# Fused attention and two feed-forward blocks on one Trainium2 core: other places in the order for weight conversions, a constant row and the splits of the values

## The chip, the cores and the metric

One core of one Trainium2 chip. The metric is the device time of one execution in microseconds (us); lower is better. Before the change it was 958.23 us, the median of three runs (957.24 to 959.21).

## The reference

Attention with rotary positions on 4 batches x 8 heads x 576 tokens x 64, then a gated block (512 to 1024, split into u and v, v normalised and mixed over the tokens), then a block with a low-rank mixing over the tokens (U: 576x32, V: 32x576) and a 512-2048-512 pair of layers. All is float32.

```
q_rot, k_rot = (rotate(q), rotate(k))
scores = scale * np.matmul(q_rot, k_rot.transpose(0, 1, 3, 2))
scores = scores - np.max(scores, axis=-1, keepdims=True)
attn = np.exp(scores)
attn = attn / (np.sum(attn, axis=-1, keepdims=True) + 1e-09)
attn_out = np.matmul(attn, v)
...
h = gelu_tanh(x @ w_in)
u, v = (h[..., :d_ff // 2], h[..., d_ff // 2:])
v_n = (v - mu) / np.sqrt(var + 1e-06) * g_ln
v_s = np.einsum('ts,bsd->btd', w_sg, v_n) + b_sg[None, :, None]
x = x + (u * v_s) @ w_out
...
u = x + (x.transpose(0, 2, 1) @ U @ V).transpose(0, 2, 1)
out = u + np.maximum(u @ w_ch1, 0.0) @ w_ch2
```

## The kernel before

Every float32 product is built from two TensorE operands of a shorter format: a high part (ScalarE copies the tensor into it) and a low part (the tensor less its high part). The weights arrive as 64-bit floats and are converted in place by `from_f64` (L66): one ScalarE operation (Abs) and four VectorE operations (L72 to L75) per chunk, then a ScalarE copy for the high part and a GpSimd subtraction for the low part.

**The attention** is written out by hand on all five engines. It runs in slots: slot t does the scores of chunk t % 5 of head t // 5 (`scores`: keys in chunks of 128, all 576 queries), the values product of slot t - 3 (`values`), row maxima 12 slots ahead (`row_max`), and then whatever was put down for slot t by `later`. 32 heads make 160 slots; some 20 slots lie before slot 0. Each engine does its part of the slots in order.

- Scores are two matmul pairs per chunk: one tile pair stacks a high part over a low one, the other (65 rows) pairs a high part with a low one, and its 65th row is -1 against the row of the maxima, so that the maximum is subtracted on TensorE. Before, tile K2 is `rot - K1` over all 128 partitions (L166), which overwrites the row of -1, so a memset on GpSimd (L172) writes it again for each head.
- For head h: rope on GpSimd in slots 5h-26, 5h-25 and 5h-23 (L147 to L149), the high part on ScalarE with a DMA in 5h-20 (L161, L163), the low part on GpSimd with two DMAs in 5h-17 (L166 to L168), the memset in 5h-11 (table `LEAD`).
- `row_max`: VectorE reduces scores in PSUM to a maximum (L220, five per head); there are three PSUM tiles for these and the scores together.
- Chunk 4 has 64 keys: its exponentials (L251) are split into a high part (L253, ScalarE) and a low part `ph` (L255, VectorE), and so are its values (`value_stacks`, L180 on ScalarE and L181 on GpSimd, per head).
- After the second head of pair i, from slot t0 = 10i + 12 on (`finish`): the row sums are collected by DMA (t0), 1e-9 is added on GpSimd (`guard`, L306, t0+5), VectorE inverts (L309, t0+7), two DMAs spread the result (t0+8, t0+11), and VectorE multiplies both heads (`apply`, L324, t0+24 and t0+26) (table `INVERSE`).
- Eight chunks of w_in, one of U and two of V are loaded 10 slots apart from slot 15 on (`MATRIX`, `APART`), and converted 15 slots after their load (`CONVERT`): Abs, then VectorE's four operations in four successive slots, then the high and the low part.

**Behind the attention** only TensorE's order is written by hand; a scheduler places the others. The gated block of batch 0 has v steps, u steps, four s steps (token mixing; their result g goes through VectorE L622 and L623, ScalarE L624, GpSimd L506), the v steps of batch 1, and four o steps (output matmul `w`, residual on VectorE L634), then the transposes `t` (L646) of the low-rank mixing, which is the first to use U4 and V4. `other_weights` (L522) converts w_out in four pieces, one per `next(ow)`; its raw tiles borrow the buffers YH and YL of the later steps.

Of the kernel before, what the change touches and what calls it, by code (L numbers as in the profile page):

```python
# [52 lines left out]
def tile_kernel(ctx: ExitStack, tc: tile.TileContext, qk, vv, tabs, w_in, g_ln, wsgT, b_sg, w_out, u_r, v_r, w1, w2, out):  # L53
# [123 lines left out]
    def value_stacks(h):  # L177
        VS = VSs[h % 4]
        src = VVs[(h // 2) % 3][:, SPLIT, h % 2, :D]
        later(max(NC * h - SPLIT_V[0], SPLIT_V_FIRST[0]), lambda: nc.scalar.activation(VS[:, 0, :, :D], src, AF.Copy))  # L180
        later(max(NC * h - SPLIT_V[1], SPLIT_V_FIRST[1]), lambda: (nc.gpsimd if h > 1 else nc.vector).tensor_tensor(VS[:, 1, :, :D], src, f(VS[:, 0, :, :D]), ALU.subtract))  # L181

    def first_stacks(h):
# [11 lines left out]
        def high():  # L195
            e = BY_ACT[h]
            copy(e[0], Q1[z], rot[z])
            copy(e[1], Q1[a], rot[z])
            copy(e[2], K1[a], rot[a])
            copy(e[3], K1[z], rot[a])  # L200
            copy(e[4], Q2[a, 0:S], rot[z])
# [713 lines left out]
```

## Time and profile before

| | |
|---|---|
| time, median of 3 runs | 958.23 us (957.24 to 959.21) |
| the profiled execution: its time | 957.72 us |
| its span in the profile | 955.9 us |
| granted TensorE clock, mean | 0.989 of full speed |
| TensorE busy (matmul) | 927.9 us, 97% |
| weight loads | 784.5 us, 82% |
| VectorE busy | 542.5 us, 57% |
| ScalarE busy | 346.8 us, 36% |
| GpSimd busy | 409.9 us, 43% |

The span is the part of the profiled execution that the profiler covers; its own time is 1.8 us longer. A matmul counts as busy while it waits in the pipe for an operand or for PSUM, so 97% is not the share of useful work. The attention takes about the first 311 us; VectorE's and GpSimd's work lies mostly there.

### The profile page before, as it was taken

What the parts mean: (1) busy time and instruction counts of PE and PEld (TensorE: products, weight loads), DVE (VectorE), ACT (ScalarE), POOL (GpSimd) and SP (SyncE); (2) the same over time, 40 slices, a digit from 0 to 9 for tenths busy, and PEclk for the clock granted to TensorE, in tenths of its full rate; (3) what the DMA queues carried; (4) which work ended last, traced back from release to release, by engine and by line L of the source; (5) the groups of instructions that cost most, each with busy time, mean ns of one, the idle gap of its engine ahead of it and who ended that gap; (6) DMA issues with size and microseconds to landing.
All of it is one profiled execution on the core that took longest, in us unless ns stands there. A gap on an engine that the chain in (4) does not pass through costs nothing.

```text
span 955.9 us, 13163 instructions
## 1 busy us (share of the span) xinstructions
PE 927.9 (97%) x5179; PEld 784.5 (82%) x5180; DVE 542.5 (57%) x721; ACT 346.8 (36%) x550; POOL 409.9 (43%) x352
## 2 busy tenths in 40 slices
PE   5899999999999999999999899999999999999998
PEld 2588777777887888999999787888888888888887
DVE  7766899999874486334338845642642552222222
ACT  4356666666656443313225322311220320101000
POOL 7787999999943485231417533210210220000000
PEclk7899999999999999999999999999999999999999
DMA  5477776776630500000003001320220210000112
GB/s 176 127 206 201 210 206 182 207 191 173 168 90 14 164 25 1 1 1 19 5 23 111 22 23 46 109 67 1 88 88 1 67 45 0 1 1 23 45 48 86
DMA packets 57301, 77.93 MB, mean 82 GB/s; under 512 B 29756, under 2 KB 33111, under 8 KB 57239
## 3 DMA queue, kind: packets, MB, share of 16 engines
q1 hardware_dynamic: 56928, 77.01, 28.7%
q8 instruction: 41, 0.67, 0.3%
q14 instruction: 22, 0.17, 0.1%
q10 hardware_dynamic: 310, 0.08, 0.0%
HBM read 55.02 MB, written 4.79 MB: 63 GB/s over the span
## 4 chain that ended last, share of the span: by engine, by line
PE 74%; DVE 17%; issue 3%; DMA 2%; POOL 2%; ACT 1%; SPq 0%; ACTq 0%; DVEq 0%; POOLq 0%
PE a L542 21%; PE r L542 20%; PE pv L272 10%; PE st L244 6%; PE w L542 5%; DVE MX L220 4%; PE m L542 3%; PE sm L215 3%; PE u L542 3%; PE v L542 3%; DVE ph L255 2%; DVE t L74 1%; DVE t L72 1%; DVE X L324 1%; DVE t L75 1%
## 5 line engine op out<-in xcount | busy, mean ns | idle before, releaser
L272 PE MATMUL pv<-pc,VV 128*65 128x288 f32 x512 | 144.7, 405 | 0.5 <-DVE sums L293 0.5
L220 DVE TENSOR_REDUCE MX<-sm 128x1 f32<-128x576 f32 (+1 forms) x160 | 117.6, 751 | 36.5 <-PE sm L215 33.6
L244 PE MATMUL st<-Q,K 65*128 65x288 f32 (+3 forms) x640 | 126.5, 320 | 1.6 <-DVE MX L220 1.2
L735 DVE SCALAR_TENSOR_TENSOR RL<-r,RH 128x1024 fp32r<-128x1024 f32 (+1 forms) x38 | 42.3, 1112 | 123.8 <-ACT RH L734 123.7
L734 ACT ACTIVATE RH<-r 128x1024 fp32r<-128x1024 f32 (+1 forms) x38 | 35.6, 936 | 207.2 <-PE r L542 207.2
L244 PEld LDWEIGHTS st<-Q,K 65*128 65x128 f32 (+3 forms) x640 | 95.6, 179 | 16.2 <-DVE MX L220 5.4
L750 DVE TENSOR_TENSOR X<-a,X 128x256 f32<-128x256 f32 (+4 forms) x65 | 46.4, 745 | 90.8 <-PE a L542 90.7
L247 ACT ACTIVATE pc<-st 128x576 f32<-128x576 f32 x128 | 82.8, 648 | 36.5 <-PE st L244 31.1
L542 PE MATMUL a<-RH,setB 128*128 128x512 f32 (+1 forms) x320 | 93.3, 368 | 0.0
L272 PEld LDWEIGHTS pv<-pc,VV 128*65 128x65 f32 x512 | 68.5, 136 | 29.5 <-DVE sums L293 0.7
L215 PE MATMUL sm<-K,Q 128*128 128x288 f32 (+1 forms) x320 | 76.8, 325 | 12.8 <-ACT Q L191 6.9
L542 PE MATMUL a<-RH,setA 128*128 128x512 f32 (+1 forms) x288 | 83.8, 367 | 0.0
L542 PE MATMUL r<-UH,setA 128*128 128x512 f32 (+1 forms) x256 | 73.1, 364 | 0.1
L542 PE MATMUL r<-UH,setB 128*128 128x512 f32 (+1 forms) x256 | 73.2, 363 | 0.0
L215 PEld LDWEIGHTS sm<-K,Q 128*128 128x128 f32 (+1 forms) x320 | 52.5, 184 | 20.2 <-ACT Q L191 7.4
L542 PEld LDWEIGHTS a<-RH,setB 128*128 128x128 f32 x320 | 58.2, 189 | 10.0
L506 POOL TENSOR_TENSOR setB<-t,setB 128x512 fp32r<-128x512 f32 x16 | 20.7, 1294 | 102.9 <-ACT setB L695 91.8
L542 PEld LDWEIGHTS a<-RH,setA 128*128 128x128 f32 x288 | 52.1, 188 | 9.0
L542 PE MATMUL a<-RL,setB 128*128 128x512 f32 (+1 forms) x160 | 58.9, 368 | 0.0
L148 POOL TENSOR_TENSOR raw<-raw,tab 128x576 f32<-128x576 f32 x31 | 54.5, 1760 | 5.6 <-DMA raw<-in_qk 5.6
L506 POOL TENSOR_TENSOR setA<-t,setA 128x512 fp32r<-128x512 f32 x16 | 21.5, 1352 | 73.7 <-ACT setA L695 69.9
L542 PEld LDWEIGHTS r<-UH,setA 128*128 128x128 f32 x256 | 46.1, 188 | 8.2 <-DVE X L676 0.4
(170 smaller groups left out, 2030.3 us busy)
## 6 DMA issues: line engine op xcount, KB each, us to landing
raw<-in_qk SPq DMA_DIRECT2D x31, 576.0 KB, 4.8
raw<-in_w SPq DMA_DIRECT2D x24, 512.0 KB, 3.6
Q<-K SPq DMA_DIRECT2D x29, 288.0 KB, 3.5
VV<-in_vv SPq DMA_DIRECT2D x16, 320.0 KB, 3.9
rb<-rr SPq DMA_DIRECT2D x15, 288.0 KB, 3.7
Q<-K SPq DMA_DIRECT2D x29, 144.0 KB, 2.4
K<-K SPq DMA_DIRECT2D x29, 144.0 KB, 2.4
raw<-in_w_in SPq DMA_DIRECT2D x8, 512.0 KB
```

Source lines behind the costliest of these rows:

```text
L148: lambda: e.tensor_tensor(raw[:, 1], raw[:, 1], tab[:, 1], ALU.mult),
L215: nc.tensor.matmul(ps[:TS[t], n, :HALF], Q1[:, t * P:t * P + TS[t]], K1[:, n * HALF:(n + 1) * HALF], start=True, stop=True)
L220: nc.vector.tensor_reduce(MXs[h % 2][:TS[t], t:t + 1], ps[:TS[t], :, :HALF], AX.XY, ALU.max)
L244: nc.tensor.matmul(ps[:kk, n, :HALF], l[:, c * P:c * P + kk], r[:, ns], start=st, stop=not st)
L247: nc.scalar.activation(h2(pc[:kk]), ps[:kk, :, :HALF], AF.Exp, scale=0.125)
L255: lows.append(lambda: nc.vector.tensor_tensor(ph[D:], pt, f(ph[:D]), ALU.subtract))
L272: nc.tensor.matmul(o, l, r, start=(c == 0 and j == 0), stop=(c == NC - 1 and j == len(pr) - 1))
L506: return nc.gpsimd.tensor_tensor(out, a, b, ALU.subtract)
L542: nc.tensor.matmul(o, l, rr, start=(j == 0), stop=(j == n - 1))
L734: nc.scalar.activation(RH[:, s], ps[:, :, :WIDE[blk]], AF.Relu)
L735: nc.vector.scalar_tensor_tensor(RL[:, s], ps[:, :, :WIDE[blk]], 0.0, f(RH[:, s]), ALU.max, ALU.subtract)
L750: nc.vector.tensor_tensor(X[b][:, e2, xs], ps[:, :n, us], X[b][:, e2, xs], ALU.add)
```

## The change

- Chunks of w_in stand 15 slots apart (`APART` 10 to 15), and only they are converted in the attention. U and V are converted in the gated block, as three more steps of `other_weights`: U with the fourth s step of batch 0, V's halves with the first two v steps of batch 1.
- k and q change roles: the kept tile with 65 rows (K2) now holds a high part that comes by DMA into 64 rows, and its row of -1 stays, so the memset per head is gone from head 5 on. The low part goes to Q2, whose 65th row is then overwritten by the row of maxima.
- The values of chunk 4 are split for both heads of a pair at once.
- The 1e-9 is added on VectorE, directly ahead of the inversion.
- A pair whose multiplications would fall into the slots of a chunk's conversion (`BUSY`) is multiplied at t0+19 and t0+21 in place of t0+24 and t0+26.

```diff
-LEAD = 26, 25, 23, 20, 17, 11
+LEAD = 26, 25, 23, 20, 17
...
-INVERSE = 5, 7, 8, 11, (24, 26)
+INVERSE = 7, 8, 11, (24, 26), (19, 21)
-MATRIX, APART, CONVERT, ROWS = 15, 10, 15, (151, 159)
+MATRIX, APART, CONVERT, ROWS = 15, 15, 15, (151, 159)
...
-    K1s = [p1.tile([P, S], F32R, name=f"K1_{i}") for i in range(NS)]
-    Qs = [p1.tile([P, S + NC * P], F32R, name=f"Q_{i}") for i in range(NS)]
-    Q1s = [t[:, :S] for t in Qs]
-    Q2s = [t[:D + 1, S:] for t in Qs]
-    K2s = [p1.tile([P, S], F32R, name=f"K2_{i}") for i in range(NS)]
+    Q1s = [p1.tile([P, S], F32R, name=f"Q1_{i}") for i in range(NS)]
+    Ks = [p1.tile([P, 2 * S], F32R, name=f"K_{i}") for i in range(NS)]
+    K1s = [t[:, :S] for t in Ks]
+    K2s = [t[:D + 1, S:] for t in Ks]
+    Q2s = [p1.tile([P, NC * P], F32R, name=f"Q2_{i}") for i in range(NS)]
...
         def low():
-            nc.gpsimd.tensor_tensor(K2, rot, f(K1), ALU.subtract)
-            nc.sync.dma_start(f(Q1[z]), f(K2[z]))
-            nc.sync.dma_start(f(K1[z]), f(K1[a]))
+            nc.gpsimd.tensor_tensor(Q2[:, :S], rot, f(Q1), ALU.subtract)
+            nc.sync.dma_start(f(K1[z]), f(Q2[z, :S]))
+            nc.sync.dma_start(f(Q1[z]), f(Q1[a]))
...
-            steps = rope(nc.gpsimd, h) + (high, low, lambda: nc.gpsimd.memset(f(K2[D:D + 1]), -1.0))
+            steps = rope(nc.gpsimd, h) + (high, low)
+            if h < NS:
+                steps += lambda: nc.gpsimd.memset(f(K2[D:]), -1.0),
...
     def value_stacks(h):
-        VS = VSs[h % 4]
-        src = VVs[(h // 2) % 3][:, SPLIT, h % 2, :D]
+        if h % 2:
+            return
+        VS = VSs[h // 2 % 2]
+        src = VVs[(h // 2) % 3][:, SPLITS[0], :, :D]
...
-        def guard():
-            nc.gpsimd.tensor_scalar_add(rc, rc, 1e-9)
-
         def invert():
+            nc.vector.tensor_scalar_add(rc, rc, 1e-9)
             nc.vector.reciprocal(rc, rc)
...
-                later(t0 + (INVERSE[4][a] if i < NP - 2 else 16 + a), lambda a=a: apply(a))
+                tick = t0 + INVERSE[4 if t0 + INVERSE[3][0] in BUSY else 3][a]
+                later(tick if i < NP - 2 else t0 + 16 + a, lambda a=a: apply(a))
...
-    def u_chunk(t0):
...
-    def v_chunk(t0, a):
...
+    BUSY = {MATRIX + APART * i + CONVERT + j for i in range(2 * KT) for j in range(1, 5)}
...
+        t = staged(p2, u_r, "YH", n=NC * 32).rearrange("p (c r) -> p c r", r=32)
+        for j in (0, 2, 3):
+            nc.scalar.activation(U4[:, :, j], t, AF.Copy)
+        less(U4[:, :, 1], t, f(U4[:, :, 0]))
+        yield
+        for a in range(2):
+            hs = slice(a * HALF, (a + 1) * HALF)
+            t = staged(p2, v_r[:, 2 * a * HALF:2 * (a + 1) * HALF], ("YL", "YH")[a], n=HALF)
+            nc.scalar.activation(V4[:, hs], t, AF.Copy)
+            less(V4[96:, hs], t[96:], f(V4[96:, hs]))
+            yield
...
-        run(v_step, n, 0, 1)
+        for t in range(2):
+            v_step(n, t)
+            next(ow, None)
```

GpSimd's order over two heads in the middle of the attention, before (raw is the rope's tile, setA a weight, VS the values' split, K the tiles of k):

```order
L172 MEMSET K_3_107 1x576
L147 TENSOR_TENSOR raw_89<-raw_89,tab 128x576
L148 TENSOR_TENSOR raw_89<-raw_89,tab 128x576
L350 TENSOR_TENSOR setA_74<-t_155,setA_73 128x512
L149 TENSOR_TENSOR raw_89<-raw_89 128x576
L306 TENSOR_SCALAR rc_1303<-rc_1303 128x9
L166 TENSOR_TENSOR K_0_104<-raw_92,K_0_94 128x576
L181 TENSOR_TENSOR VS_114<-VV_111,VS_114 128x64
```

The second head is the same without the lines of setA and rc. Now a head with a chunk and one without:

```order
L147 TENSOR_TENSOR raw_92<-raw_92,tab 128x576
L148 TENSOR_TENSOR raw_92<-raw_92,tab 128x576
L352 TENSOR_TENSOR setA_76<-t_147,setA_75 128x512
L149 TENSOR_TENSOR raw_92<-raw_92 128x576
L166 TENSOR_TENSOR Q_4_108<-raw_91,Q_4_98 128x576
L147 TENSOR_TENSOR raw_89<-raw_89,tab 128x576
L148 TENSOR_TENSOR raw_89<-raw_89,tab 128x576
L149 TENSOR_TENSOR raw_89<-raw_89 128x576
L166 TENSOR_TENSOR Q_0_104<-raw_92,Q_0_94 128x576
L185 TENSOR_TENSOR VS_114<-VV_111,VS_114 128x2x64
```

The memset and the sums' addition (rc) are gone, the values' split comes once for two heads, and a weight's subtraction once for three. On VectorE the slots of the table give over six heads: chunk, pair, pair, chunk, neither, pair; before it was chunk and pair in turn.

VectorE's order in the gated block of batch 0, from the last w_out piece to the statistics of batch 1's first v tiles, before (t is a tile being converted, g the gated product, m the s step's PSUM):

```order
L75 SCALAR_TENSOR_TENSOR t_3779<-YL,t_3779 128x512
L622 SCALAR_TENSOR_TENSOR g<-m_3_3788,gh,bh 128x576
L623 TENSOR_TENSOR g<-g,ug 128x576
L585 BN_STATS bst<-gt 128x6 x2
L586 BN_AGGR bmv<-bst 128x2 x2
```

and now, where two L75 of 128x288 and then the statistics follow the last row:

```order
L72 TENSOR_SCALAR t_3726<-t_3726 128x160
L73 TENSOR_SCALAR t_3726<-t_3726 128x160
L74 SCALAR_TENSOR_TENSOR t_3726<-YH,t_3726 128x160
L618 SCALAR_TENSOR_TENSOR g<-m_3_3691,gh,bh 128x576
L75 SCALAR_TENSOR_TENSOR t_3726<-YH,t_3726 128x160
L619 TENSOR_TENSOR g<-g,ug 128x576
L72 TENSOR_SCALAR t_3751<-t_3751 128x288
L72 TENSOR_SCALAR t_3790<-t_3790 128x288
L73 TENSOR_SCALAR t_3751<-t_3751 128x288
L73 TENSOR_SCALAR t_3790<-t_3790 128x288
L74 SCALAR_TENSOR_TENSOR t_3751<-YL,t_3751 128x288
L74 SCALAR_TENSOR_TENSOR t_3790<-YH,t_3790 128x288
```

Three operations of U stand ahead of the last g, one inside it, and all eight of V behind it, ahead of the statistics. ScalarE's order at the same place, now (GH is the high part of g, gt the gelu of v; before, the rows of U, t and V were not there):

```order
L510 ACTIVATE WOH<-t_3682 128x512
L515 ACTIVATE U_79<-t_3726 128x5x32 x3
L620 ACTIVATE GH<-g 128x576
L71 ACTIVATE t_3751<-YL 128x288
L71 ACTIVATE t_3790<-YH 128x288
L529 ACTIVATE gt<-v_0_3737 128x1024
L521 ACTIVATE V_80<-t_3751 128x288
L521 ACTIVATE V_80<-t_3790 128x288
L589 ACTIVATE VH<-gt 128x512 x2
```

GpSimd has the subtraction of U ahead of the low part of the last g, and those of V ahead of the variance of the v tiles.

## Rows read from the trace of the kernel before

**Rows 1.** Busy time of each engine in stretches: us, then engines, clock, DMA share, GB/s.
```profile
150.00:200.00 50.00, 49.38 (x289) 38.89 (x290) 49.50 (x61) 32.33 (x57) 48.44 (x41) 1.00 0.75 202
...
340.00:368.00 28.00, 25.98 (x160) 23.57 (x158) 25.91 (x26) 11.73 (x21) 20.26 (x14) 1.00 0.00 1
```

**Rows 2.** Timeline of ScalarE: the exponential of chunk 4, heads 0, 8, 22 and 28.
```profile
40.76 0.64 ACT L251 ACTIVATE pt<-st 64x576 f32<-64x576 f32 x1 [0.95 <-PE st L244]
...
108.61 0.64 ACT L251 ACTIVATE pt<-st 64x576 f32<-64x576 f32 x1 [1.12 <-PE st L244]
...
233.64 0.64 ACT L251 ACTIVATE pt<-st 64x576 f32<-64x576 f32 x1 [1.12 <-PE st L244]
...
284.54 0.64 ACT L251 ACTIVATE pt<-st 64x576 f32<-64x576 f32 x1 [1.12 <-PE st L244]
```

**Rows 3.** Timeline of TensorE's weight loads, 180 to 190 us, those that waited.
```profile
184.81 0.46 PEld L272 LDWEIGHTS pv<-ph,VS 128*65 128x65 f32 x4 [0.48 <-DVE ph L255]
185.60 0.57 PEld L244 LDWEIGHTS st<-Q,K 128*128 128x128 f32 x4 [0.33 <-DVE MX L220]
188.62 0.45 PEld L244 LDWEIGHTS st<-Q,K 128*64 128x64 f32 x4 [0.41 <-DVE MX L220]
```

**Rows 4.** VectorE's groups by form, 100 to 270 us: busy us, mean ns, idle before.
```profile
L220 DVE TENSOR_REDUCE MX<-sm 128x1 f32<-128x576 f32 x78 | 57.3, 752 | 5.4 <-PE sm L215 4.4
L255 DVE TENSOR_TENSOR ph<-pt,ph 64x576 fp32r<-64x576 f32 x20 | 31.5, 1574 | 0.6
L324 DVE TENSOR_TENSOR X<-stage,rb 64x576 f32<-64x576 f32 x19 | 22.7, 1193 | 0.3
...
L72 DVE TENSOR_SCALAR t<-t 128x512 f32<-128x512 f32 x7 | 10.6, 1508 | 0.0
L75 DVE SCALAR_TENSOR_TENSOR t<-raw,t 128x512 uint32<-128x512 uint32 x7 | 7.3, 1046 | 0.0
L73 DVE TENSOR_SCALAR t<-t 128x512 uint32<-128x512 uint32 x7 | 7.1, 1014 | 0.0
...
L74 DVE SCALAR_TENSOR_TENSOR t<-raw,t 128x512 uint32<-128x512 uint32 x7 | 4.7, 675 | 0.0
...
L72 DVE TENSOR_SCALAR t<-t 128x160 f32<-128x160 f32 x1 | 1.5, 1504 | 0.0
...
L73 DVE TENSOR_SCALAR t<-t 128x288 uint32<-128x288 uint32 x2 | 0.9, 451 | 0.0
L73 DVE TENSOR_SCALAR t<-t 128x160 uint32<-128x160 uint32 x1 | 0.8, 782 | 0.0
L75 DVE SCALAR_TENSOR_TENSOR t<-raw,t 128x160 uint32<-128x160 uint32 x1 | 0.7, 675 | 0.0
L74 DVE SCALAR_TENSOR_TENSOR t<-raw,t 128x160 uint32<-128x160 uint32 x1 | 0.3, 317 | 0.0
```

**Rows 5.** Timelines of VectorE and of GpSimd, 55 to 95 us.
```profile
84.65 0.75 DVE L255 TENSOR_TENSOR ph<-pt,ph 64x576 fp32r<-64x576 f32 x1
...
86.35 1.41 POOL L166 TENSOR_TENSOR K<-raw,K 128x576 fp32r<-128x576 f32 x1 [1.81 <-ACT K L161]
```

**Rows 6.** GpSimd's groups by form, 100 to 270 us: busy us, mean ns, idle before.
```profile
L350 POOL TENSOR_TENSOR setA<-t,setA 128x512 fp32r<-128x512 f32 x7 | 12.5, 1790 | 0.0
L172 POOL MEMSET K<- 1x576 f32 x20 | 11.4, 572 | 1.2
...
L306 POOL TENSOR_SCALAR rc<-rc 128x9 f32<-128x9 f32 x9 | 5.9, 659 | 0.8
```

**Rows 7.** Timeline of TensorE's weight loads, 365 to 402 us, two that waited.
```profile
370.00 0.30 PEld L542 LDWEIGHTS w<-GL,WOH 128*128 128x128 f32 x2 [1.51 <-POOL GL L506]
381.25 1.40 PEld L646 LDWEIGHTS t<-ident,X 128*128 128x128 f32 x13 [0.76 <-DVE X L634]
```

**Rows 8.** Timeline of VectorE, 340 to 382 us, statistics and the last residual addition.
```profile
369.09 1.29 DVE L585 BATCH_NORM_STATS2 bst<-gt 128x6 f32<-128x512 f32 x2 [1.67 <-ACT gt L533]
...
380.44 0.76 DVE L634 TENSOR_TENSOR X<-w,X 128x576 f32<-128x576 f32 x1 [0.96 <-PE w L542]
```

More of the change, by code (lines that the diff above doesn't have):

```diff
@@ L133, in tile_kernel @@
     SPLITS = list(range(NC))[SPLIT]
-    VSs = [p1.tile([P, 2, len(SPLITS), D + 1], F32R, name=f"VS_{i}") for i in range(4)]
+    VSs = [p1.tile([P, 2, 2, D + 1], F32R, name=f"VS_{i}") for i in range(2)]
     def load(h):
@@ L160, in high @@
         def high():
-            nc.scalar.activation(K1, rot, AF.Copy)
-            both = f(Qs[h % NS][a, :2 * S]).rearrange("p (a s) -> p a s", a=2)
-            nc.sync.dma_start(both, f(K1[z]).rearrange("p (a s) -> p a s", a=1).to_broadcast([D, 2, S]))
+            nc.scalar.activation(Q1, rot, AF.Copy)
+            both = f(Ks[h % NS][a]).rearrange("p (a s) -> p a s", a=2)
+            nc.sync.dma_start(both, f(Q1[z]).rearrange("p (a s) -> p a s", a=1).to_broadcast([D, 2, S]))
         def low():
-            nc.gpsimd.tensor_tensor(K2, rot, f(K1), ALU.subtract)
-            nc.sync.dma_start(f(Q1[z]), f(K2[z]))
-            nc.sync.dma_start(f(K1[z]), f(K1[a]))
+            nc.gpsimd.tensor_tensor(Q2[:, :S], rot, f(Q1), ALU.subtract)
+            nc.sync.dma_start(f(K1[z]), f(Q2[z, :S]))
+            nc.sync.dma_start(f(Q1[z]), f(Q1[a]))
         if h < len(BY_ACT):
@@ L177, in value_stacks @@
     def value_stacks(h):
-        VS = VSs[h % 4]
-        src = VVs[(h // 2) % 3][:, SPLIT, h % 2, :D]
-        later(max(NC * h - SPLIT_V[0], SPLIT_V_FIRST[0]), lambda: nc.scalar.activation(VS[:, 0, :, :D], src, AF.Copy))
-        later(max(NC * h - SPLIT_V[1], SPLIT_V_FIRST[1]), lambda: (nc.gpsimd if h > 1 else nc.vector).tensor_tensor(VS[:, 1, :, :D], src, f(VS[:, 0, :, :D]), ALU.subtract))
+        if h % 2:
+            return
+        VS = VSs[h // 2 % 2]
+        src = VVs[(h // 2) % 3][:, SPLITS[0], :, :D]
+        later(NC * h - SPLIT_V[0], lambda: nc.scalar.activation(VS[:, 0, :, :D], src, AF.Copy))
+        later(NC * h - SPLIT_V[1], lambda: (nc.gpsimd if h else nc.vector).tensor_tensor(VS[:, 1, :, :D], src, f(VS[:, 0, :, :D]), ALU.subtract))
     def first_stacks(h):
@@ L196, in high @@
             e = BY_ACT[h]
[L197 to L201, printed above, removed]
+            copy(e[0], K1[z], rot[z])
+            copy(e[1], K1[a], rot[z])
+            copy(e[2], Q1[a], rot[a])
+            copy(e[3], Q1[z], rot[a])
+            copy(e[4], K2[a], rot[z])
         def low():
-            nc.vector.tensor_tensor(Q1[z], rot[z], f(Q1[z]), ALU.subtract)
-            nc.vector.tensor_tensor(K2[a], rot[a], f(K1[a]), ALU.subtract)
+            nc.vector.tensor_tensor(K1[z], rot[z], f(K1[z]), ALU.subtract)
+            nc.vector.tensor_tensor(Q2[a, :S], rot[a], f(Q1[a]), ALU.subtract)
         value_stacks(h)
@@ L240, in scores @@
         ps = psp.tile([P, 2, 512], F32, tag="ss", name=f"st{h}_{c}", bufs=3)
-        for l, r, st in ((K1, Q1, True), (K2[0:D + 1], Q2, False)):
+        for l, r, st in ((K1, Q1, True), (K2, Q2[:D + 1], False)):
             for n in range(2):
@@ L328, in finish @@
         later(t0, collect)
-        for tick, fn in zip(INVERSE, (guard, invert, gather, spread)):
+        for tick, fn in zip(INVERSE, (invert, gather, spread)):
             later(t0 + tick, fn)
@@ L391, in tile_kernel @@
         nc.gpsimd.memset(MXs[i], 0.0)
-    for i in range(4):
+    for i in range(2):
         nc.gpsimd.memset(f(VSs[i][:, 0, :, D:]), 1.0)
@@ L407, in tile_kernel @@
         later(NC * h - LOAD - NC * (h > 2 * NR), lambda h=h: load(h))
-    WTICK = [MATRIX + APART * i for i in range(2 * KT + 3)]
     for i in range(2 * KT):
-        w_in_chunk(WTICK[i], i)
-    u_chunk(WTICK[2 * KT])
-    for a in range(2):
-        v_chunk(WTICK[2 * KT + 1 + a], a)
+        w_in_chunk(MATRIX + APART * i, i)
     def x_hi(b, k):
@@ L877, in swap @@
         return np.concatenate([x[:, :, D // 2:], x[:, :, :D // 2]], axis=2)
-    x = [t.transpose(0, 1, 3, 2) for t in (k, q)]
+    x = [t.transpose(0, 1, 3, 2) for t in (q, k)]
     qk = np.stack([np.concatenate(x, axis=2), np.concatenate([swap(t) for t in x], axis=2)], axis=2)
```

28 lines of the change are left out of this document (8 added, 20 removed).

## The prediction, made before the changed kernel ran

> **What bounds the kernel now.** I read the stretch table first. In the middle of the attention TensorE, VectorE and GpSimd are all busy for about 49 of 50 us [rows 1], so shares don't say which one sets the pace. The spacing of one instruction that comes once per head does: the exponential of chunk 4 on ScalarE, whose starts are the heads' clock [rows 2]. Over heads 0 to 8 it comes every (108.61 - 40.76) / 8 = 8.48 us, and again every 8.48 us over heads 22 to 28. The 14 periods between take 125.03 us, where 14 x 8.485 are 118.79: 6.24 us are lost there. They are lost in seven heads of 9.3 to 9.4 us, heads 9, 11, 13, 15, 17, 19 and 21; all others of that stretch keep 8.5.
>
> What TensorE waits for in such a head stands in its weight loads: 0.48 us for the low part of the probabilities (ph), then 0.33 and 0.41 us for row maxima that have yet to free a PSUM buffer, all VectorE's [rows 3]. So VectorE is late, and the reader should see why in its durations [rows 4]. A head costs it five maxima (5 x 0.75 = 3.76 us) and ph (1.57). A weight chunk adds 1.51 + 1.01 + 0.68 + 1.05 = 4.24, and the two multiplications that normalise a pair add 2 x 1.19 = 2.39. Two heads with a chunk and a pair make 10.66 + 4.24 + 2.39 = 17.3 us, and the small cast and reciprocal fill it to the 17.9 that such a pair of heads takes; TensorE alone would need 17.0. VectorE is full, and short by 0.9 us each time: 7 times.
>
> Its durations are themselves stretched. ph took 0.75 us at 84.65, when GpSimd stood idle for 1.81 us until ScalarE gave it the next head's high part [rows 5], and 1.57 us on average later, when GpSimd never stood idle. Beside a GpSimd that is always busy, VectorE's operations on two SBUF tensors take about twice as long.
>
> **The change, part by part.**
>
> *GpSimd in the attention.* Per two heads it loses two memsets (2 x 0.57), the guard (0.66) and, with chunks every three heads, a third of a chunk's subtraction (1.79 / 3 = 0.60) [rows 6]; one split of values fewer per pair is left as a reserve. That is 2.4 of some 17.9 us, 13%. Its idle time then comes back where it was before the chunks began: ahead of the low part, whose release by ScalarE is fixed, and that is when ph runs.
>
> *VectorE in the attention.* Over six heads it now has two chunks and three pairs: 6 x 5.33 + 2 x 4.24 + 3 x 2.39 = 47.6 us at the stretched prices, and with casts, reciprocals and the three guards (between nothing and the 0.66 that GpSimd took, taken as 0.2 since VectorE's durations are the shorter ones) about 50; TensorE needs 50.9. It is tight where heads stand chunk, pair, pair, chunk: 4 x 5.33 + 8.48 + 4.78 + casts and reciprocals of about 1.5 = 36.1 against 33.9. If ph falls back to between 0.75 us and halfway there (1.16), which I take since GpSimd's idle time lies there, these four heads are 4 x 0.4 to 0.8 shorter and fit, but for 0.6 at most, which is less than a chunk head alone runs over unpunished (1.1, below). Then all seven stalls go: **-6.2 us**. The least gain is that of the second rival.
>
> *Rows of -1, exchange of the roles of k and q, splits per pair.* TensorE issues the same matmuls on the same shapes, the DMAs of the stacks keep their number and size, and ScalarE, idle for 1.1 us before every chunk-4 exponential [rows 2], loses 16 small copies. The head start before slot 0 keeps its order on VectorE, which sets it. I cost these at nothing; what covers them is TensorE's own 8.48 us.
>
> *The guard of the last pair* now stands before its reciprocal on VectorE, and the load of the spatial weights is queued on SP behind the transfer of that reciprocal. TensorE waits for these weights, so it is on the path: +0.2, at most the 0.66 it took on GpSimd.
>
> *The low-rank weights in the gated block.* Here VectorE is the engine that is late: 25.9 of 28 us busy from 340 to 368, GpSimd 20.3 [rows 1]. TensorE waits for the low part of the last g, 1.51 us at 370.00, and for the last residual addition, 0.76 us at 381.25 [rows 7]. Both waits get longer.
> First, three conversions of U stand ahead of the last g and the fourth inside it. The four took 1.50 + 0.78 + 0.32 + 0.68 = 3.28 us in the attention [rows 4]; the one that was not held up took 0.317, so 4 x 0.317 = 1.3 is the lower end. GpSimd is busy for 72% here against 97% there, so I take a value nearer the lower end: +1.9. The three copies of U on ScalarE run beside the rest of g, and the subtraction of U on GpSimd ends before the last high part of g reaches it.
> Second, the eight conversions of V stand ahead of the statistics of the next batch's first v tiles. Before, VectorE idled 1.67 us there (ScalarE's copy of g, 0.7, then the gelu, 1.0) [rows 8]. Now it waits 0.7, then 0.45 for the first absolute value, then runs 8 x 0.451 = 3.6 [rows 4]: 4.75 in place of 1.67, so 3.1 later. Everything behind is a chain through VectorE, GpSimd, ScalarE's next gelu and back to the last addition, which had 0.96 us in hand [rows 8]: +2.1 on TensorE's wait for that addition. At 0.82, the mean of the four 128x160 rows, eight cost 6.6, so +5.1; if the gaps swallow them, 0. Together **+4.0**, from 1.3 to 8.4.
> The three loads go to SP after its last attention transfer, into buffers that are free before they are needed, and hold up nothing there. Later blocks keep their order.
>
> *The sum.* The profiled execution took 957.72 us, 0.5 less than the median of the runs, 958.23. 957.72 - 6.24 + 0.2 + 4.0 = 955.7; as a median 956.2.
>
> **The rivals.**
>
> *The conversions are hidden.* VectorE has gaps behind the last g (1.67 and 0.96 in the rows), and if the V conversions fit in such gaps only the lower end of U is left: 957.72 - 6.24 + 0.1 + 1.3 = 952.9, as a median 953.4. For it: GpSimd has little to do there, so nothing stretches them. Against it: they stand in VectorE's order ahead of the statistics, whether there is a gap or not.
>
> *The stretch stays.* GpSimd still runs four long operations per head, and if each two-input operation of VectorE keeps meeting one, the four heads chunk, pair, pair, chunk are 2.1 to 2.2 us too long. A chunk head alone runs 3.76 + 1.57 + 4.24 = 9.6, 1.1 over, before TensorE has to wait; so each such group costs between 1.0 and 2.1, say 1.5. There are four groups (eight chunks), 6.0 in all, which leaves 0.2 of the 6.24: 957.72 - 0.2 + 0.2 + 4.0 = 961.7, as a median 962.2, slower than before. It decides from the point at which ph's mean stays above about 1.4 us. Beside it stands a rule of the Trainium skill (SBUF — State Buffer, section Who interferes with whom): a VectorE instruction with two SBUF inputs contends with a GpSimd instruction that reads SBUF, not with one that only writes, and whichever starts first holds the ports to its end. By that rule the memsets that go never held VectorE up, and only the time they free counts. The trace agrees as far as it goes: the doubling of ph is there, but no row separates memsets from the rest. Against the rival: between 40 and 100 us, with the memsets still there, GpSimd had begun to wait for ScalarE, and ph fell to 0.75.
>
> **How the numbers follow.** A measurement of this kernel can tell 0.2%, 1.9 us: faster is under 956.3, slower over 960.1. The forecast (stalls gone, block 2 to 8.4 us longer) has 0.62, its middle just under the border: 0.29 faster, 0.30 no change, 0.03 slower. Hidden conversions 0.22, all faster. The stretch stays 0.16: 0.06 no change, 0.10 slower. The range goes from the first rival, 953.0, to the upper end of the block's price, 957.72 - 6.24 + 0.2 + 8.4 + 0.5 = 960.6; cases of both signs hold chances, but the forecast's own range, 954.0 to 960.6, is nearly all of it.
>
> **What would show it.** Right: 8.48 us between the chunk-4 exponentials of all heads from 0 to 28, ph's mean under 1.2 us there, GpSimd idle ahead of the low part, and in the gated block longer waits of TensorE for the low part of the last g and for the last residual addition of the first batch. Wrong: heads over 9 us behind the chunks at heads 9, 15, 21 and 27 (the second rival), or these two waits unchanged (the first). A wait of TensorE in the attention for anything but VectorE would be something I have not seen.

## The result, the profile after, and where the time went

The changed kernel took 962.96 us, the median of five runs (962.11 to 964.29); the kernel before, run beside it, 957.72 (955.94 to 959.21). The ratio is 1.0056 (95% interval 1.0040 to 1.0072), 5.4 us slower. The profiled execution took 962.11 us, its span 960.3.

| | before | after |
|---|---|---|
| first to last chunk-4 exponential (31 periods of the attention) | 266.91 us | 268.15 us |
| last chunk-4 exponential to the end of the span | 648.2 us | 651.7 us |
| VectorE busy | 542.5 us | 530.6 us |
| GpSimd busy | 409.9 us | 376.1 us |

Both engines that were full do less work, and both parts of the kernel are longer.

**The attention.** The clock of the heads, as in [rows 2], is the chunk-4 exponential on ScalarE (L255 now). Its timeline in the changed kernel, heads 7, 8 and 9:

```profile
99.94 0.64 ACT L255 ACTIVATE pt<-st 64x576 f32<-64x576 f32 x1 [1.10 <-PE st L248]
...
110.25 0.64 ACT L255 ACTIVATE pt<-st 64x576 f32<-64x576 f32 x1 [1.64 <-PE st L248]
...
118.89 0.64 ACT L255 ACTIVATE pt<-st 64x576 f32<-64x576 f32 x1 [1.12 <-PE st L248]
```

From 99.94 to 110.25 are 10.31 us, and 8.64 follow; where 8.5 is the rule, 2.0 are lost. The same comes in heads 14, 20 and 26 (10.29, 10.31 and 9.75), 7.2 us together. The seven heads of 9.4 us are gone: their 6.2 us were swapped for 7.2 in four places. Behind a chunk stand two heads with a pair's multiplications, and the long head is the second of the two.

VectorE's groups by form from 100 to 270 us, beside [rows 4] (busy us, mean ns, idle before):

```profile
L224 DVE TENSOR_REDUCE MX<-sm 128x1 f32<-128x576 f32 x78 | 57.8, 755 | 16.5 <-PE sm L219 14.8 <-PE sm L222 0.3
L325 DVE TENSOR_TENSOR X<-stage,rb 64x576 f32<-64x576 f32 x21 | 30.0, 1426 | 0.3
L259 DVE TENSOR_TENSOR ph<-pt,ph 64x576 fp32r<-64x576 f32 x19 | 19.8, 1042 | 0.7
...
L72 DVE TENSOR_SCALAR t<-t 128x512 f32<-128x512 f32 x6 | 6.5, 1090 | 0.0
```

ph (L259) fell from 1574 to 1042 ns, as was forecast, and L72 from 1508 to 1090. But the multiplications of the pairs (L325) rose from 1193 to 1426, and the mean hides where the long ones lie. GpSimd's groups of the same stretch, beside [rows 6]:

```profile
L166 POOL TENSOR_TENSOR Q<-raw,Q 128x576 fp32r<-128x576 f32 x19 | 30.1, 1583 | 8.3 <-ACT Q L161 8.3
...
L352 POOL TENSOR_TENSOR setA<-t,setA 128x512 fp32r<-128x512 f32 x6 | 7.6, 1273 | 24.6 <-ACT setA L351 21.0 <-DMA Q<-Q 3.6
```

GpSimd stands idle 33 us here, and where it does so is new: 21.0 us ahead of the chunk's subtraction (L352), which waits for ScalarE's high copy of the chunk, and only 8.3 ahead of the low part (L166).

The bad head itself, VectorE's timeline:

```profile
100.21 1.90 DVE L325 TENSOR_TENSOR X<-stage,rb 64x576 f32<-64x576 f32 x1
...
103.01 0.39 DVE L309 TENSOR_SCALAR rc<-rc 128x9 f32<-128x9 f32 x1
103.44 0.22 DVE L310 RECIPROCAL rc<-rc 128x9 f32<-128x9 f32 x1
103.69 1.79 DVE L259 TENSOR_TENSOR ph<-pt,ph 64x576 fp32r<-64x576 f32 x1
```

GpSimd's timeline of the same time:

```profile
95.15 1.28 POOL L352 TENSOR_TENSOR setA<-t,setA 128x512 fp32r<-128x512 f32 x1 [4.65 <-ACT setA L351]
...
100.09 1.41 POOL L147 TENSOR_TENSOR raw<-raw,tab 128x576 f32<-128x576 f32 x1
...
103.45 1.41 POOL L149 TENSOR_TENSOR raw<-raw 128x576 f32<-128x576 f32 x1
```

TensorE's weight loads that waited in it:

```profile
105.53 0.46 PEld L275 LDWEIGHTS pv<-ph,VS 128*65 128x65 f32 x4 [0.81 <-DVE ph L259]
106.32 0.56 PEld L248 LDWEIGHTS st<-Q,K 128*128 128x128 f32 x4 [0.33 <-DVE MX L224]
```

The first multiplication (X) begins at 100.21, 0.12 behind a rope operation on GpSimd (100.09), and takes 1.90. The guard and the reciprocal follow, and ph begins at 103.69, 0.24 behind the next rope operation (103.45): 1.79 in place of 0.75, and TensorE waits 0.81 for it. Ahead of all that GpSimd had stood for 4.65 us; its work then ran on without a gap from 95.15 to 111.5, across both pair heads.

**The gated block.** What [rows 7, 8] showed, in the changed kernel; first TensorE's weight loads:

```profile
371.24 0.30 PEld L538 LDWEIGHTS w<-GL,WOH 128*128 128x128 f32 x2 [1.20 <-POOL GL L491]
...
383.59 0.14 PEld L642 LDWEIGHTS t<-ident,X 128*128 128x128 f32 x1 [1.07 <-DVE X L630]
...
384.92 1.40 PEld L642 LDWEIGHTS t<-ident,X 128*128 128x128 f32 x13 [0.53 <-DVE X L630]
```

Then VectorE (U's conversions, the first of V's, the statistics):

```profile
364.94 0.23 DVE L72 TENSOR_SCALAR t<-t 128x160 f32<-128x160 f32 x1
365.21 0.24 DVE L73 TENSOR_SCALAR t<-t 128x160 uint32<-128x160 uint32 x1
365.49 1.46 DVE L74 SCALAR_TENSOR_TENSOR t<-YH,t 128x160 uint32<-128x160 uint32 x1
...
370.07 1.50 DVE L72 TENSOR_SCALAR t<-t 128x288 f32<-128x288 f32 x2 [1.11 <-ACT t L71]
...
373.41 1.28 DVE L581 BATCH_NORM_STATS2 bst<-gt 128x6 f32<-128x512 f32 x2
```

U's four conversions took 0.23, 0.24, 1.46 and (behind a piece of g) 0.70 us. V's began 1.11 us after VectorE fell idle and ran until 373.41, when the statistics followed. The wait for the low part of g did not get longer (1.20 against 1.51), but the wait for the last residual additions, 0.76 before, is now 1.07 and twice 0.53.

### The profile page after: what moved, and what is told of

The parts are those of the page before. It is cut to its first block, busy times and chain, and to the rows that moved or that the text cites. A ratio compares the mean times of both kernels' runs of the same rounds, so it can differ in the third digit from the quotient of the medians.

```text
span 960.3 us, 12969 instructions
## 1 busy us (share of the span) xinstructions
PE 927.2 (97%) x5179; PEld 783.6 (82%) x5180; DVE 530.6 (55%) x736; ACT 345.5 (36%) x534; POOL 376.1 (39%) x290
## 4 chain that ended last, share of the span: by engine, by line
PE 75%; DVE 12%; POOL 4%; issue 3%; DMA 3%; ACT 1%; SPq 0%; ACTq 0%; POOLq 0%; DVEq 0%
PE a L538 21%; PE r L538 20%; PE pv L275 10%; PE st L248 6%; PE v L538 4%; PE w L538 4%; PE m L538 3%; PE sm L219 3%; PE u L538 3%; DVE MX L224 2%; DMA K<-Q 2%; DVE t L74 1%; DVE g L619 1%; POOL Q L166 1%; DVE t L75 1%
## 5 line engine op out<-in xcount | busy, mean ns | idle before, releaser
L248 PE MATMUL st<-Q,K 65*128 65x288 f32 (+3 forms) x640 | 124.5, 317 | 2.0 <-DVE MX L224 1.0
L166 POOL TENSOR_TENSOR Q<-raw,Q 128x576 fp32r<-128x576 f32 x29 | 45.1, 1554 | 23.4 <-ACT Q L161 23.2
L148 POOL TENSOR_TENSOR raw<-raw,tab 128x576 f32<-128x576 f32 x31 | 52.0, 1677 | 5.5 <-DMA raw<-in_qk 5.5
L538 PE MATMUL a<-RL,setA 128*128 128x512 f32 (+1 forms) x144 | 52.9, 368 | 0.0
```

What stands on the lines that cost most here:

```text
L148: lambda: e.tensor_tensor(raw[:, 1], raw[:, 1], tab[:, 1], ALU.mult),
L166: nc.gpsimd.tensor_tensor(Q2[:, :S], rot, f(Q1), ALU.subtract)
L248: nc.tensor.matmul(ps[:kk, n, :HALF], l[:, c * P:c * P + kk], r[:, ns], start=st, stop=not st)
L538: nc.tensor.matmul(o, l, rr, start=(j == 0), stop=(j == n - 1))
```

## The experiments

All runs, in the order in which they stand below. The attention is the stretch from the first to the last chunk-4 exponential of the profiled execution; the median is of the runs, the ratio that to the kernel before on the same chip, whose medians were 956.3 to 957.5 us. Differences between two runs are those of their ratios, times 957.5 us; by the two intervals such a difference is uncertain by some 1.3 to 2.5 us.

| run | edit | attention, us | median, us | ratio (95% interval) |
|---|---|---|---|---|
| x1 | changed kernel, chunk's subtraction two slots later | 272.65 | 967.07 | 1.0101 (1.0085 to 1.0116) |
| x3 | changed kernel, U and V in the last heads | 268.22 | 958.43 | 1.0013 (1.0004 to 1.0022) |
| x4 | x1 and x3 | 272.73 | 962.97 | 1.0063 (1.0046 to 1.0080) |
| x5 | kernel before, U and V in the gated block | 266.92 | 960.52 | 1.0032 (1.0022 to 1.0043) |
| x6 | changed kernel, guard and reciprocal behind ph | 262.89 | 955.24 | 0.9982 (0.9974 to 0.9991) |
| x7 | x1 and x6 | 262.04 | 955.82 | 0.9985 (0.9977 to 0.9994) |
| x8 | x1, high copy a slot later | 267.24 | 960.18 | 1.0040 (1.0018 to 1.0061) |
| y3 | x4, x6 and x8, X adjacent | 269.84 | 961.80 | 1.0054 (1.0041 to 1.0068) |
| x10 | changed kernel, guard on GpSimd again | 261.43 | 954.42 | 0.9979 (0.9963 to 0.9995) |
| y1 | x3 and x6 | 262.95 | 954.48 | 0.9973 (0.9964 to 0.9983) |
| y5 | x4 and x6 | 262.13 | 954.32 | 0.9967 (0.9955 to 0.9979) |
| y6 | y5, X adjacent | 266.59 | 958.71 | 1.0015 (1.0007 to 1.0024) |
| z2 | kernel before, guard on VectorE | 265.20 | 955.25 | 0.9983 (0.9971 to 0.9994) |
| z1 | x3 and x10 | 261.47 | 952.07 | 0.9948 (0.9931 to 0.9965) |

### Is it GpSimd's bunched work? (x1)

```diff
-            later(t0 + CONVERT + j, fn)
+            later(t0 + CONVERT + (8 if j == 6 else j), fn)
```

> The changed kernel, with one instruction elsewhere: GpSimd's subtraction of each weight chunk stands two slots later, behind the rope (L149) and the low part (L166) of the next heads in place of ahead of them. Theory A (GpSimd, now early, waits 4.6 us for ScalarE's high copy of the chunk, and everything behind it runs without a gap into the two pair heads behind): that wait shrinks to under 1.5 us each, heads 8, 14, 20 and 26 come back from 10.3 (9.75 for head 26) to at most 8.7 us, and the time falls by 5 to 7 us against the changed kernel's 963, to about 957. Theory B (two pair heads behind a chunk head hold more of VectorE's work than TensorE leaves time for, wherever GpSimd's subtraction stands): these heads keep at least 1.5 us of loss each and the time falls by at most 2, to 961 or more.

The time went a third way: 4.3 us slower than the changed kernel. The wait for the chunk's copy was gone, and GpSimd's idle time (46.7 us from 60 to 270) lay ahead of the low part, just where the prediction had wanted it. Ten heads lost 0.9 to 1.5 us each, every second one from 8 to 26: those that have the guard and the reciprocal ahead of ph, whether chunk or pair stand in them or neither. Head 10, in VectorE's timeline, then GpSimd's and TensorE's weight loads:

```profile
121.48 0.15 DVE L309 TENSOR_SCALAR rc<-rc 128x9 f32<-128x9 f32 x1
...
121.91 1.64 DVE L259 TENSOR_TENSOR ph<-pt,ph 64x576 fp32r<-64x576 f32 x1
```

```profile
121.53 1.41 POOL L166 TENSOR_TENSOR Q<-raw,Q 128x576 fp32r<-128x576 f32 x1 [1.98 <-ACT Q L161]
```

```profile
123.61 0.45 PEld L275 LDWEIGHTS pv<-ph,VS 128*65 128x65 f32 x4 [0.92 <-DVE ph L259]
```

The low part begins as soon as ScalarE has released it, at 121.53. ph begins 0.38 us later, takes 1.64, and TensorE waits 0.92. GpSimd was idle until just before ph. From this came theory C: what counts is whether ph begins ahead of the GpSimd operation beside it or behind its start.

### U and V back in the attention, and the block alone (x3, x4, x5)

x3 puts the two loops of the kernel before back, at slots 128, 141 and 150 (behind the last chunk of w_in), and takes the three steps out of `other_weights`:

```diff
         w_in_chunk(MATRIX + APART * i, i)
+    u_chunk(128, 16)
+    v_chunk(141, 0, 12)
+    v_chunk(150, 1, 10)
...
-        t = staged(p2, u_r, "YH", n=NC * 32).rearrange("p (c r) -> p c r", r=32)
...
```

The second and third numbers are the slots from load to conversion. x5 is the reverse: in the kernel before, only these steps move into the gated block.

> The changed kernel, with U and V converted in the last heads of the attention again (behind the last weight chunk) in place of the gated block. If the gated block's price is what the traces show (the block is 2.7 us longer than before, and 0.4 more behind it): 2.7 to 3.5 us less than the changed kernel's 963, about 960, and the four long heads of the attention stay. If the price lies in the reordered attention alone: no change. If the conversions stretch the tail of the attention: less than 1.5 us gained, and new heads over 9 us from head 26 on.

> Both edits together, the later subtraction of each weight chunk on GpSimd and U and V converted in the last heads of the attention. If both theories hold the gains add: 957.7 of before, less the 6.2 of its stalled heads, plus up to 1 for what else moved, so 952 to 954. If theory B holds: 958 to 960.

> The kernel before, with one part of the change alone: U and V are converted in the gated block, all else stays (weight chunks 10 slots apart, memset per head, guard on GpSimd). This gives the price of that part by itself. If it is what the block shows in the changed kernel: 2.7 to 3.1 us slower than before, with the same waits (TensorE for the low part of the last g, 1.2 us, and for the residual addition, 1.5 us), and the attention unchanged. By the prediction's estimate 4.0 us slower; its lower rival 1.3.

x3 is 4.1 us better than the changed kernel with the attention unchanged, somewhat more than expected (2.7 to 3.5, within the uncertainty); x4 is 3.6 better than x1 and, since x1's edit costs here too, slower than both of its forecasts. x5 is the clean price: 1.0032, so 3.1 us (2.1 to 4.1). Where it arises, TensorE's matmuls that waited in the gated block of x5:

```profile
341.43 0.53 PE L550 MATMUL m<-WSL,VH 128*128 128x288 f32 x2 [0.89 <-POOL WSL L503]
...
367.97 0.53 PE L550 MATMUL w<-GH,WOH 128*128 128x288 f32 x2 [1.60 <-ACT GH L632]
369.46 0.53 PE L550 MATMUL w<-GL,WOH 128*128 128x288 f32 x2 [0.96 <-POOL GL L503]
...
377.44 0.53 PE L550 MATMUL w<-GH,WOH 128*128 128x288 f32 x2 [0.80 <-ACT gt L541]
...
381.80 0.33 PE L654 MATMUL t<-ident,X 128*128 128x128 f32 x1 [0.81 <-DVE X L642]
382.47 0.33 PE L654 MATMUL t<-ident,X 128*128 128x128 f32 x1 [0.33 <-DVE X L642]
383.13 1.64 PE L654 MATMUL t<-ident,X 128*128 128x128 f32 x13 [0.34 <-DVE X L642]
```

and those that waited there in the kernel before:

```profile
341.81 0.53 PE L542 MATMUL m<-WSH,VH 128*128 128x288 f32 x2 [1.01 <-ACT WSH L516]
343.34 0.54 PE L542 MATMUL m<-WSL,VH 128*128 128x288 f32 x2 [1.01 <-POOL WSL L506]
...
370.00 0.54 PE L542 MATMUL w<-GL,WOH 128*128 128x288 f32 x2 [1.27 <-POOL GL L506]
...
381.25 1.64 PE L646 MATMUL t<-ident,X 128*128 128x128 f32 x13 [0.53 <-DVE X L634]
```

For g these are 1.60 + 0.96 against 1.27, 1.3 longer; for the gelu and the residual additions 0.80 + 0.81 + 0.33 + 0.34 against 0.53, 1.75 longer. But these sums are not yet the prices of U and V. Further ahead TensorE waits for the spatial weights (WSH, WSL), 1.01 + 1.01 us before and only 0.89 in x5, so the matmuls on the low part of the last g begin no later than before: 62.27 us behind the last chunk-4 exponential in x5, 62.33 in the kernel before, 62.62 in the changed kernel. So at that point U has cost next to nothing, or in x5 the shorter wait hides it (why that wait is shorter was not tried). The pair of x10 and z1 says the same: 62.67 with U in the block, 62.83 with U in the attention. From these matmuls to the last row of transposes TensorE takes 381.25 - 370.00 = 11.25 us before, 383.13 - 369.46 = 13.67 in x5 and 384.92 - 371.24 = 13.68 in the changed kernel, so this stretch, in which V's conversions lie, is 2.4 longer. What is left of the 3.1 lies behind, or within the interval.

### Who begins first (x6, x7, x8)

x6, and x7 with x1's edit: the reciprocal, with the guard, a slot later and so behind ph.

```diff
-INVERSE = 7, 8, 11, (24, 26), (19, 21)
+INVERSE = 8, 9, 11, (24, 26), (19, 21)
```

x8: x1's edit and `LEAD = 26, 25, 23, 19, 17`.

> The changed kernel, with the guard and the reciprocal behind ph in VectorE's order in place of ahead of it (slot t0+8, the transfer of the result one slot later too). New theory C, from the trace of the run with the later subtraction: what counts is whether ph (0.75 us) starts ahead of the GpSimd operation that runs beside it or behind its start; behind it, ph lasts until that operation's end and 0.65 longer (1.6 to 1.9 us). In the changed kernel's head 8 the guard and the reciprocal took 0.68 us ahead of a ph that began 0.24 us behind a rope operation. By C ph begins first there, lasts 0.75, and the long heads lose about 1 of their 1.8 us: 4 x 1, so about 959 against 963. By A alone (GpSimd's bunched work, whatever the order on VectorE): less than 1 us gained.

> The later subtraction and the guard and reciprocal behind ph, together. In the run with the later subtraction alone (967), heads 8, 10 and 12 of every six each lost 1 to 1.5 us, and in each ph began 0.1 to 0.4 us behind the start of the low part on GpSimd (L166). By theory C the two of the three that have the guard ahead of ph (heads 8 and 12, 14 and 18, ...) come back to 8.5, head 10, 16, 22 stays at 9.4: 967 - 3 x 1.2 - 4 x 1.2 = about 958 to 960. By theory B (VectorE has too much to do there): 965 or more.

> The later subtraction, and ScalarE's high copy of each head (L161) one slot later in its order, so that the low part on GpSimd (L166), which it releases, starts about 1.7 us later and ph, even when VectorE is late, comes first. By theory C ph is near 0.75 us in all heads, and the heads that lost 1 to 1.5 us in the run with the later subtraction alone (ten of them, 12 us in all) return to 8.5: about 955 to 957. If the same work only meets another VectorE operation and the lost time stays lost (theory B): 964 or more. If the later high copy is itself too late for the scores: longer heads everywhere, over 970.

x6 is 7.1 us better than the changed kernel, more than expected; 5.3 of them lie in the attention. Its long heads are 8.92 to 8.95 us in place of 9.75 to 10.31. The same head as above, VectorE and then GpSimd:

```profile
100.47 1.90 DVE L325 TENSOR_TENSOR X<-stage,rb 64x576 f32<-64x576 f32 x1
...
103.37 0.87 DVE L259 TENSOR_TENSOR ph<-pt,ph 64x576 fp32r<-64x576 f32 x1
```

```profile
100.34 1.41 POOL L147 TENSOR_TENSOR raw<-raw,tab 128x576 f32<-128x576 f32 x1
101.71 1.92 POOL L148 TENSOR_TENSOR raw<-raw,tab 128x576 f32<-128x576 f32 x1
103.71 1.81 POOL L149 TENSOR_TENSOR raw<-raw 128x576 f32<-128x576 f32 x1
```

ph now begins 0.34 us ahead of the rope operation L149, in the last 0.26 us of the one before it (L148), and takes 0.87; it is L149 that gets longer. X still begins 0.13 behind L147 and takes 1.90, which leaves 0.47 of the 2.0 us lost per group. So the place of the guard and the reciprocal ahead of ph was most of the loss, and GpSimd's bunched work, unchanged here, was not enough for it. x7 came to 955.8, better than its forecast, and no head of it is over 8.7 us (head 10 has the guard too, so it came back with the others, which the expectation had wrong): the idle time ahead of the low part, which made x1 the slowest run, does no harm once ph is early.

x8 came to 960.2, between its forecasts, and refutes the plain form of theory C, that a later low part sets ph free. ph's mean fell only to 1.03 us (x1: 1.25), and L73 and L74 rose from 1.21 and 0.96 to 1.31 and 1.23. TensorE's weight loads waited 1.4 us for ph from 60 to 270 us (x1: 8.1), but still 4.9 for maxima (x1: 5.6). GpSimd's work had been pushed onto other operations of VectorE.

### The part undone (x10), and the sums (y1, y5, y3, y6)

x10 undoes one part of the change:

```diff
+        def guard():
+            nc.gpsimd.tensor_scalar_add(rc, rc, 1e-9)
+
         def invert():
-            nc.vector.tensor_scalar_add(rc, rc, 1e-9)
...
+        later(t0 + 5, guard)
```

y1 and y5 add x6's edit to x3 and x4; y6 puts the multiplications (24, 26), (19, 21) at (24, 25), (19, 20) besides; y3 is y6 with x8's edit.

> The changed kernel with one part undone: 1e-9 is added on GpSimd again (slot t0+5), so that on VectorE only the reciprocal stands ahead of ph. By theory C (ph must start before the GpSimd operation beside it): in head 8 ph began at 103.69, 0.24 us behind the rope operation on GpSimd, with 0.39 us of guard ahead of it; without the guard it begins first and lasts 0.75, so the four long heads fall from 10.3 to 9.0 or less, and the time to about 956 to 958. By theory A (bunched work on GpSimd, now 0.66 us more per pair): 962 or more.

> The changed kernel with two edits: U and V converted in the last heads of the attention, and the guard and the reciprocal behind ph. Alone they gave 4.5 and 7.7 us against the changed kernel's 963. They lie in different stretches, so they should add: 963.0 - 4.5 - 7.7 = 950.8 (950 to 952). If the tail of the attention, now reached sooner, takes back some: 953.

> As the one before, with the later subtraction of each chunk as well. With the guard behind ph that edit shortened the attention by another 0.9 us (starts 39.69 to 301.73 against 40.72 to 303.61), though the medians did not show it (955.8 and 955.2): 950 to 951.5, and no head over 8.7 us. By theory A it must be at least 1 us better than the one before.

> As the one before, with the two multiplications of a pair in adjacent slots in place of two apart, so that the second is done sooner before ph. By theory C it changes at most 1 us in either direction, since ph already comes first; if it piles both on the row maxima of one slot: 1 to 3 us slower, with TensorE waiting for maxima.

> All edits that the theories ask for: U and V converted in the last heads of the attention (4.5 us less in the run with that alone), the later subtraction, the guard and the reciprocal behind ph, the high copy one slot later, and the two multiplications of a pair in adjacent slots in place of two apart. By theory C no head over 8.7 us up to head 28: 958.4 of the run with U and V alone, less the 7.2 us of its four long heads, so 951 to 952. By theory B: 957 or more.

x10 is 0.9979 of before, some 7.4 us better than the changed kernel (6.7 of them in the attention), and has no head over 8.7 us. Head 8, VectorE and GpSimd:

```profile
99.66 0.98 DVE L327 TENSOR_TENSOR X<-stage,rb 64x576 f32<-64x576 f32 x1
...
101.54 0.19 DVE L312 RECIPROCAL rc<-rc 128x9 f32<-128x9 f32 x1
101.77 0.77 DVE L259 TENSOR_TENSOR ph<-pt,ph 64x576 fp32r<-64x576 f32 x1
```

```profile
94.60 1.28 POOL L355 TENSOR_TENSOR setA<-t,setA 128x512 fp32r<-128x512 f32 x1 [4.65 <-ACT setA L354]
...
97.86 0.24 POOL L309 TENSOR_SCALAR rc<-rc 128x9 f32<-128x9 f32 x1
...
99.98 1.94 POOL L147 TENSOR_TENSOR raw<-raw,tab 128x576 f32<-128x576 f32 x1
101.88 1.94 POOL L148 TENSOR_TENSOR raw<-raw,tab 128x576 f32<-128x576 f32 x1
```

The wait of 4.65 us and the work behind it without a gap are still there; theory A falls. Two starts have changed: X begins 0.32 us ahead of the rope operation, which the guard on GpSimd has put back, and takes 0.98; ph begins 0.11 ahead of the next, as the last one ends, and takes 0.77. The rows tell the two shifts apart. Counted from the start of the chunk's subtraction, X begins at 5.06 us in both kernels, and the rope operation at 5.38 here against 4.94 in the changed kernel: that X is short is GpSimd's doing. ph begins only 0.11 us ahead of the next rope operation, so a guard of 0.39 ahead of it would have put it behind (an estimate from these rows): that ph is short needs the guard off VectorE. X is 0.92 us and ph 1.02 shorter than in the changed kernel, together nearly the 2.0 us that were lost there. How much of x10's gain each shift makes by itself was not run; x6, with GpSimd's order untouched, gives most to ph.

y1 and y5 came to 954.5 and 954.3 where 951 was expected, though their attention is as short as x6's and x7's: what is missing lies behind it, where y1's conversions in the attention give 0.9 us over x6 and not the 4.1 of x3. Why was not settled. y6 and y3 missed widely. In y6 heads 10, 16 and 22 take 9.87 us. The first of these in y6, VectorE, GpSimd, TensorE's weight loads:

```profile
120.25 1.97 DVE L259 TENSOR_TENSOR ph<-pt,ph 64x576 fp32r<-64x576 f32 x1
```

```profile
120.20 1.42 POOL L166 TENSOR_TENSOR Q<-raw,Q 128x576 fp32r<-128x576 f32 x1 [1.99 <-ACT Q L161]
```

```profile
122.28 0.45 PEld L275 LDWEIGHTS pv<-ph,VS 128*65 128x65 f32 x4 [0.92 <-DVE ph L259]
```

and the same head in y5, VectorE and GpSimd:

```profile
119.66 0.75 DVE L259 TENSOR_TENSOR ph<-pt,ph 64x576 fp32r<-64x576 f32 x1
```

```profile
120.13 1.55 POOL L166 TENSOR_TENSOR Q<-raw,Q 128x576 fp32r<-128x576 f32 x1 [1.06 <-ACT Q L161]
```

0.47 us ahead of the low part, ph takes 0.75; 0.05 us behind its start, 1.97, and the head is 1.4 us longer.

### Does the guard cost by itself? (z2), and the best version (z1)

z2 moves the guard alone in the kernel before: x10's diff the other way. z1 is x10 with x3's edit.

> The kernel before, with one part of the change alone: the guard moves from GpSimd to VectorE, directly ahead of the reciprocal and of ph. If the guard ahead of ph costs by itself (0.15 to 0.4 us per pair where VectorE is late): the seven stalled heads of 9.4 become 9.6 to 9.8, and the time is 1 to 3 us longer. If GpSimd's 0.66 us per pair, which it gives back, count for more there: the stalls shrink and the time falls by 1 to 3 us, and then the guard hurts only in the changed kernel's order, where GpSimd has a free choice of when to begin.

> The changed kernel with the two parts undone that the runs showed to cost: the guard is on GpSimd again, and U and V are converted in the last heads of the attention. If what is left of the change is its gain alone: 954.4 of the run with the guard undone, less the 2.3 to 3 us by which the block is longer, so 951.5 to 952.5. If the block gives it back, as with the guard behind ph (954.5 where 950.8 was expected): 953.5 to 954.5.

z2 is 0.9983 of before: in the old order, where seven heads lose time anyway, the guard on VectorE even helps a little (ph's mean falls from 1479 to 1252 ns from 60 to 270 us, and the seven heads lose 0.4 us each in place of 0.9). That GpSimd is rid of it would explain this, but was not tried apart. Of the orders tried, the move costs only in the changed kernel's. z1 has the lowest time of all: 952.07 us, 0.9948 of before, the change's gain in the attention without the two parts that gave it back; its interval still overlaps that of y5. Here U and V in the attention are worth 3.0 over x10, as x5 had priced them.

## Why the prediction was wrong

It forecast 956.2 us and a faster kernel; it is 963.0 and slower.

- **What bounds the kernel: right.** VectorE is late, because GpSimd stretches its operations. The runs make the stretching exact (below).
- **The stalls go, -6.24: wrong, and this is the step that failed.** The attention became 1.2 us longer. The prediction added up VectorE's work by mean prices, put the three guards in at 0.2 us each, and concluded that chunk, pair, pair, chunk would fit since ph would fall to 1.16 or less. ph did fall, to 1.04, and the guards took 0.31 on average (60 to 270 us). But a price here is not a mean: ph takes anything from 0.75 to 2.0 us, by how much is left of a GpSimd operation that is under way when it begins. The guard's move shifted both engines in the second pair head: on VectorE it put ph 0.24 us behind the start of a rope operation, and ph took 1.79; on GpSimd, rid of the guard, a rope operation came 0.12 ahead of X, and X took 1.90. Undoing the move was worth 7.4 us (x10), putting guard and reciprocal behind ph 7.1 (x6); it had been put in at 0.2 per guard on VectorE, and as a gain of 0.66 per pair on GpSimd.
- **"Its idle time then comes back ... ahead of the low part ... and that is when ph runs": wrong twice.** It came back ahead of the chunk's subtraction; and where it did lie ahead of the low part (x1), it ended just before a late ph and did harm.
- **Rows of -1, roles of k and q, splits at nothing:** nothing speaks against it, though these parts were not undone by themselves. With the guard undone they stand, and the attention is 261.43 us, 5.5 shorter than before, near the 6.24 forecast.
- **The guard of the last pair, +0.2:** it took 0.17 us, but nothing shows that it is on the path. TensorE's matmuls on the low part of the spatial weights wait 1.42 us for it in the changed kernel, and 1.41 in x10, where the guard is on GpSimd.
- **The gated block, +4.0: right in kind, somewhat too high.** Alone it is 3.1 (2.1 to 4.1). The parts were mis-sized in opposite directions: U, taken at 1.9, shows next to nothing where g is first needed, and the stretch with V, taken at 2.1, is 2.4 longer.
- **"No row separates memsets from the rest":** one does, in the kernel before, where ph begins 0.11 us behind the start of a memset and keeps its 0.75 (VectorE, then GpSimd):

```profile
278.19 0.75 DVE L255 TENSOR_TENSOR ph<-pt,ph 64x576 fp32r<-64x576 f32 x1
```

```profile
278.08 0.57 POOL L172 MEMSET K<- 1x576 f32 x1
```

- **The second rival** named the four groups (chunk, pair, pair, chunk; the long heads came inside them, at 8, 14, 20 and 26, and not behind the last chunk at 9, 15, 21 and 27), nearly the price per group (1.5; it was 2.0 in three and 1.25 in one) and nearly the time (962.2). Its condition, ph's mean above 1.4 us, did not hold: the loss came at a mean of 1.04. A condition on a mean was the wrong test; the rows of one head, with the start times of both engines, would have been the right one.

Without the guard's move the forecast would have held: x10's ratio times the 958.2 us of the first runs is 956.2 (954.7 to 957.8). That it comes out to the tenth is luck, since the attention gains 5.5 in place of 6.24 and the block costs 3.1 in place of 4.0.

## What to carry to other kernels

Where two engines lock each other out, an operation's price is set by how much is left of the other engine's operation when it begins, so a short one placed ahead of the operation that TensorE waits for can cost many times its own length: try it behind. In another order the same move can gain (z2). Price such an edit on the timeline of the worst head, by start times of both engines, not by mean durations in a sum of busy time. An engine that is given slack moves its work in time; ask what that work will then stand beside, and undo the parts of a change one by one before giving up the whole.

## What the runs showed of the hardware

ph's duration follows one rule. From 60 to 290 us, in the timelines of all runs, a ph that begins with no GpSimd operation on two SBUF operands under way takes 0.75 to 0.76 us; one that begins during one ends 0.60 to 0.63 us behind that operation's end, whatever was left of it (0.71 twice, in x7 and y5, where 0.04 us was left). The changed kernel has 18 of the first kind and 8 of the second (1.19 to 1.80 us), x1 14 and 11 (1.64 to 2.00). X follows the same rule: 0.74 to 0.75 alone, 0.60 to 0.62 behind the other's end (changed kernel, x6, x10). The operation of GpSimd that comes second gets longer too: the rope operation beside X in x10 took 1.94 us, the same one ahead of X in the changed kernel 1.41. In the changed kernel, x1, x6 and x10, such a rope operation or low part ends 1.26 to 1.30 us behind ph or X. So either engine's operation, when it comes second, ends about its own length less 0.13 us behind the first (0.75 - 0.13 and 1.41 - 0.13; an estimate from these rows). The Trainium skill (SBUF — State Buffer, section Who interferes with whom) says that whichever begins first gets the shared ports for the whole instruction, and that the issue order decides who blocks. These traces agree.

The maxima, VectorE's reductions, took 0.75 us on average in every run, whatever GpSimd did. The guard, a VectorE operation with a single input of 128 x 9 elements, was not so steady: 0.15 us at 121.48 in x1, 0.39 in the changed kernel's head 8, and 0.81 on average in x6, where it stands behind ph. In these three runs and x7, a guard that began during a GpSimd operation on two SBUF operands ended 0.02 to 0.04 us behind its end. L72 and L73, one input as well, ran from 0.41 to 1.7 us. So operations with one input can be locked out too; the prediction spoke only of those with two. The same section says that `tensor_scalar` can contend with GpSimd in its 2-port modes. The traces agree that it is held up; in which mode it ran, no run shows.
